# Another table of engine orders for a fused attention and feed-forward kernel

## The chip, the cores and the metric

The kernel runs on one core of a Trainium2 chip. The metric is the device time in microseconds of one execution, as the median of several.

## What is computed

The reference, cut to its core:

```python
# attention: B, H, S, D = 4, 8, 768, 64; n_sink, window = 4, 64
scores = (1 / sqrt(D)) * q @ k.T
causal = rel >= 0                                # rel = query position - key position
stream_keep = causal & (is_sink | (rel < window))
mask = causal for the retrieval heads, stream_keep for the others
a = softmax(where(mask, scores, -1e9));  attn = a @ v
x = attn.transpose(0, 2, 1, 3).reshape(3072, 512)
# feed-forward: w_in [512, 2048], w_out [2048, 512]
h = x @ w_in
g = h - tanh(h)
out = g @ w_out                                  # float32 [3072, 512]
```

Which of the eight heads are retrieval heads is an input (three of them); it is read on the chip, and the masks are made from it.

## The kernel before

The 3072 tokens are worked in twelve tiles of 256, three for each batch. A tile goes through attention (transposes of q and k, scores, exp, masks, scores times v), then the hidden layer (`x @ w_in`, tanh, shrink `h - tanh(h)`), then the output layer. All data for the matmuls is float16.

The work is first recorded and then issued. Each step (four matmuls into a bank, one DVE operation, one transfer) calls `op`, which notes the engine, its expected cost and the function that issues it; there are 1653 such operations. A planner can order them, but a written table `SEQ` takes its place when it isn't empty: `follow` issues the operations in exactly that order, takes the PSUM banks from `BANK` and the lengths of the warm-up fillers from `SIZE`:

```python
for k, x in zip(self.held, BANK):
    self.bank_of[k] = (x, x + 1) if k[0] == "sc" else (x,)
self.size = SIZE
for i in self.seq[a:b]:
    self.ops[i][2]()
```

Each engine works its instructions in the order in which they were issued, so the order on TensorE (PE), VectorE (DVE), ScalarE (ACT), GpSimd (POOL) and in the transfer queues of SyncE (SP) and POOL is `SEQ` cut down to that engine. Waits between engines follow from what an operation reads and writes.

Names and lines that matter here (lines of the kernel before; the kernel after has each of them one higher from line 480 on):

- PE: L2137 `ones` are warm-up fillers, matmuls without a use, in groups with the lengths of `SIZE`. L1339 and L1342 make the matrices for each head, L1241 transposes q and k (the first three tiles), L1366 makes scores, L1450 multiplies them by v, L1546 transposes an attention result `x` (`x16_0` to `x16_3` are the four head pairs of tile 0), L1597 is the hidden layer with `win` (four quarters of w_in), L1670 and L1796 the output layer. From tile 4 on (L1796) the output layer is worked in seven block products, which need sums of blocks of g (L1763, tiles `m`) and of w_out (L1710).
- DVE: L1093 masks from the head flags; L1112 `prod` and its followers rank the heads; L1223 copies out of a bank or casts; L1422, L1404 and L1398 apply masks; L1470 and L1511 (or L1496) divide by the softmax sum; L1622 shrinks; L1763 sums; L1837, L1855 and L1867 take, fold and add the block products into the output tile `ot`.
- ACT: L1385 exp, L1611 tanh, L1221 copies and casts, L1835 takes.
- POOL: casts of q, k, v (L847, L883), the copy `vf` of v for the retrieval heads (L939), the other sums and adds, and the transfers of v, `win` and w_out into the chip.
- SP: the other loads, the transposes by DMA, and the stores of `ot`.

Which engine does an operation that more than one could do stands in small tables of letters, one string for a tile: `CASTS` the first casts of q and k, `TE` and `XE` copies after transposes, `IE` and `OE` further copies, `SUMS` (L1763), `ADDS` (L1867), `TAKES` (L1835 and L1837). D is DVE, A ACT, P POOL.

## Time and profile before

| | |
|---|---|
| median of 3 runs | 223.64 us (223.12 to 224.26) |
| the profiled execution, its own time | 222.99 us |
| its span in the profile | 221.1 us |
| PE busy | 211.8 us, 2468 matmuls |
| DVE busy | 185.8 us |
| POOL busy | 140.9 us |
| ACT busy | 134.9 us |

The span runs from the first instruction to the last; the profiled execution's own time includes what lies around it. PE's busy time includes matmuls that overlap one another at their ends. A wait is put down to what ended last before the engine went on.

### The profile page before, as it was taken

How to read it: one execution, taken by the hardware profiler on the slowest of the kernel's cores; microseconds unless marked ns; L12 is line 12 of the kernel's file. 1: busy time of each engine (PE TensorE's matmuls, PEld its weight loads, DVE VectorE, ACT ScalarE, POOL GpSimd, SP SyncE). 2: the span in 40 equal slices, each digit the busy share in tenths (PEclk: the TensorE clock that was granted, in tenths of full speed). 3: DMA queues.
4: the chain of work that ended last, by engine and by line, in shares of the span. 5: the costliest groups of instructions: out<-in, count | busy, mean ns of one | idle time of the engine just before them, and what ended most of it. 6: DMA issues, size and time to landing. Idle time of an engine off the chain costs nothing.

```text
span 221.1 us, 6568 instructions
## 1 busy us (share of the span) xinstructions
PE 211.8 (96%) x2468; PEld 174.9 (79%) x2468; DVE 185.8 (84%) x462; ACT 134.9 (61%) x214; POOL 140.9 (64%) x270
## 2 busy tenths in 40 slices
PE   7979999999999999999999999999999999999990
PEld 7657888788876675877897988989889888988880
DVE  5789978955889989798999997999897899797972
ACT  4998767885355859754675659456546774634500
POOL 8991985900899368476979999787856840030350
PEclk9999999999999999999999999999999999999999
DMA  6999999999999999999999765949244021051123
GB/s 169 178 202 201 179 175 175 197 211 245 221 187 225 221 205 241 177 233 205 216 266 202 162 144 127 231 79 183 46 89 110 3 47 50 3 142 47 52 96 104
DMA packets 112743, 34.56 MB, mean 156 GB/s; under 512 B 98882, under 2 KB 112194, under 8 KB 112706
## 3 DMA queue, kind: packets, MB, share of 16 engines
q1 hardware_dynamic: 86896, 26.75, 57.5%
q0 software_dynamic: 24992, 6.82, 30.1%
q10 hardware_dynamic: 818, 0.52, 0.8%
q8 instruction: 20, 0.33, 0.6%
q14 instruction: 17, 0.14, 0.2%
HBM read 27.26 MB, written 6.29 MB: 152 GB/s over the span
## 4 chain that ended last, share of the span: by engine, by line
PE 77%; DVE 10%; DMA 6%; ACT 3%; issue 2%; SPq 0%; DVEq 0%; POOLq 0%; POOL 0%; ACTq 0%
PE banks L1597 34%; PE banks L1796 18%; PE banks L1670 9%; PE banks L1366 7%; PE banks L1450 6%; DMA out_dram<-ot 4%; DVE gt L1622 2%; ACT pt L1385 2%; DMA rawqk<-in_k_dram 2%; DVE ot L1855 1%; DVE gu L1622 1%; ACT th L1611 1%; DVE x L1511 1%; DVE m L1763 1%; DVE QK L1223 1%
## 5 line engine op out<-in xcount | busy, mean ns | idle before, releaser
L1597 PE MATMUL banks<-xT,win 128*128 128x256 f16 x768 | 96.2, 273 | 1.3 <-DVE x L1511 1.2
L1597 PEld LDWEIGHTS <-win 128*128 128x128 f16 x768 | 72.5, 98 | 11.9 <-DMA win<-in_moe_w_in_dram 1.2
L1611 ACT ACTIVATE th<-banks 128x512 f32<-128x512 f32 x96 | 55.3, 600 | 43.3 <-PE banks L1597 34.8
L1622 DVE SCALAR_TENSOR_TENSOR gt<-th,banks 128x512 f16<-128x512 f32 x88 | 58.3, 681 | 9.1 <-ACT th L1611 8.2
L1385 ACT ACTIVATE pt<-banks 128x1024 f16<-128x1024 f32 (+3 forms) x57 | 49.3, 901 | 8.7 <-PE banks L1366 8.2
L847 POOL CAST t<-rawqk 128x256 f16 x64 | 25.7, 427 | 21.8 <-PE banks L1450 12.5
L1796 PEld LDWEIGHTS <-m 128*128 128x128 f16 x256 | 24.3, 98 | 3.2 <-issue 0.4
L1670 PE MATMUL banks<-wout,gt 128*128 128x256 f16 (+1 forms) x160 | 26.3, 294 | 0.0
L1496 DVE TENSOR_TENSOR x16t<-banks,rinv 128x128 f32 (+1 forms) x80 | 22.7, 287 | 1.5
L1763 POOL TENSOR_TENSOR m<-gt 128x512 f16<-128x512 f16 x11 | 12.7, 1156 | 17.5 <-DVE gt L1622 15.3
L1385 ACT ACTIVATE ptn<-banks 128x1024 f16<-128x1024 f32 (+1 forms) x18 | 17.2, 953 | 9.2 <-PE banks L1366 8.0
L883 POOL CAST v<-rawv 128x128 f16 x64 | 20.0, 340 | 3.0 <-DMA rawv<-in_v_dram 2.8
L1366 PE MATMUL banks<-QK 64*128 64x128 f16 (+1 forms) x343 | 20.9, 236 | 0.1
L1796 PEld LDWEIGHTS <-gt 128*128 128x128 f16 x192 | 18.2, 98 | 3.2 <-issue 0.5
L1366 PEld LDWEIGHTS <-QK 64*128 64x128 f16 x343 | 13.0, 94 | 6.7 <-issue 5.1
L1796 PE MATMUL banks<-wout,m 128*128 128x256 f16 x128 | 17.9, 273 | 0.0
L1450 PEld LDWEIGHTS <-pt 128*128 128x128 f16 x390 | 16.2, 97 | 2.1 <-issue 0.8
L1796 PE MATMUL banks<-wout,gt 128*128 128x256 f16 x128 | 17.5, 273 | 0.0
L1670 PEld LDWEIGHTS <-gt 128*128 128x128 f16 x160 | 14.2, 98 | 4.1 <-issue 0.7
L1450 PE MATMUL banks<-v,pt 128*128 128x65 f16 x208 | 16.5, 193 | 0.0
L1763 POOL TENSOR_TENSOR m<-gt,m 128x512 f16<-128x512 f16 x11 | 13.6, 1242 | 4.6 <-DVE m L1763 4.6
L1470 DVE RECIPROCAL rinv<-banks 128x4 f32<-128x4 f32 x48 | 8.3, 178 | 7.2 <-PE banks L1450 5.8
(129 smaller groups left out, 324.2 us busy)
## 6 DMA issues: line engine op xcount, KB each, us to landing
rawqk<-in_q_dram SPq DMA_DIRECT2D x18, 256.0 KB, 4.4
out_dram<-ot SPq DMA_DIRECT2D x18, 256.0 KB, 2.7
rawqk<-in_k_dram SPq DMA_DIRECT2D x17, 256.0 KB, 4.4
rawv<-in_v_dram SPq DMA_DIRECT2D x16, 256.0 KB, 4.6
win<-in_moe_w_in_dram POOLq DMA_DIRECT2D x4, 512.0 KB, 9.8
wout<-in_moe_w_out_dram POOLq DMA_DIRECT2D x4, 512.0 KB, 8.7
out_dram<-ot SPq DMA_DIRECT2D x10, 128.0 KB, 3.9
v<-in_v_dram POOLq DMA_DIRECT2D x6, 128.0 KB, 7.1
```

Of the source, the lines that this page charges most:

```text
L847: nc.gpsimd.tensor_copy(out=c5()[:, :, :, s_ : s_ + 1, :], in_=r5()[:, :, :, at, :])
L883: nc.gpsimd.tensor_copy(out=v1s[b]()[:, g * NB : g * NB + NB, RANK[s_] : RANK[s_] + 1, 0:D], in_=rw()[:, :, at, :],)
L1366: nc.tensor.matmul(out=flat[:, 512 * hh + o : 512 * hh + o + nb * 128], lhsT=lhsT, rhs=QK[p_, hp, q_0 : q_0 + nb * 128], start=not added, ...
L1385: nc.scalar.activation(out=o_, in_=i_, func=AF.Exp, scale=inv_sqrt_d)
L1450: nc.tensor.matmul(out=av()[:, i, hh, :], lhsT=pt()[:, hh, co : co + 128], rhs=vv, start=(jb == first_jb[hh]), stop=(jb == qb),)
L1496: nc.vector.tensor_mul(out=xt()[:, :, at, :], in0=av()[:, :, hh : hh + 1, 0:D], in1=rinv()[:, :, hh : hh + 1].unsqueeze(3).to_broadcast([1 ...
L1597: nc.tensor.matmul(out=ph()[:, j, :], lhsT=w_in_t[fb // 4][:, cb, f0 : f0 + 128], rhs=xT()[:, :, cb, :], start=(cb == 0), stop=(cb == HP - 1),
L1611: lambda: nc.scalar.activation(out=th()[:], in_=ph()[:], func=AF.Tanh, scale=1.0 / XS),
L1622: nc.vector.scalar_tensor_tensor(out=o_, in0=a, scalar=-XS, in1=b, op0=ALU.mult, op1=ALU.add,)
L1670: nc.tensor.matmul(out=po()[:, c0:c1], lhsT=gt()[:, f, ts * 128 : ts * 128 + 128], rhs=w_out_t[:, f, c0:c1], start=(f == 0), stop=(f == NF ...
L1763: lambda k=k, fn=fn, a=a, b=b, cs=cs, e=e: getattr(engs[e], fn)(out=S4[k][:, cs, :], in0=a()[:, cs, :], in1=b()[:, cs, :]),
L1796: nc.tensor.matmul(out=po()[:, at : at + CM], lhsT=lhs(c), rhs=rhs(c), start=c == 0, stop=c == NC - 1,)
```

## The change

`SEQ` and `BANK` are replaced as a whole, `SIZE` gets more groups (67 filler matmuls in place of 53), and the tables of letters change, which moves 62 of the 1653 operations to another engine. `SPL`, `SPT` and the 620 that becomes 450 are costs that only the planner reads; with a written `SEQ` they issue nothing and move nothing. The diff, with one row of each long table:

```diff
 SEQ = [
-    0, 1, 14, 3, 2, 4, 15, 7, 17, 5, 10, 16, 13, 18, 8, 9, 6, 11, 38, 12,
...
+    0, 1, 14, 4, 2, 10, 16, 3, 17, 7, 15, 5, 18, 8, 9, 13, 6, 38, 19, 128,
...
 BANK = [
-    7, 7, 6, 5, 4, 0, 2, 6, 2, 1, 0, 4, 5, 1, 7, 7, 2, 5, 3, 3, 1, 0, 1, 2, 4, 1, 0, 0, 0, 0, 0, 0,
...
+    7, 7, 6, 5, 4, 0, 2, 6, 0, 5, 0, 3, 4, 1, 5, 5, 2, 3, 7, 3, 7, 0, 1, 2, 3, 5, 2, 7, 1, 0, 0, 0,
...
-SIZE = {128: 20, 129: 14, 130: 11, 131: 4, 132: 4}
+SIZE = {128: 20, 129: 21, 130: 4, 131: 3, 132: 3, 133: 4, 134: 5, 135: 7}
...
-    TE = (('AA', 'AA', 'AD', 'DD'), ('AA', 'DD', 'AA', 'AA'), ('AA', 'DD', 'AD', 'DD'))
-    XE = ('DDDD', 'DAAD', 'DADA')
+    TE = (('AA', 'AA', 'AA', 'DD'), ('DD', 'AA', 'DA', 'AA'), ('AD', 'AA', 'DD', 'DD'))
+    XE = ('DADD', 'DDAA', 'DADA')
     BYD = 2
+    SPL, SPT = 18.0, 18.0
...
-    CASTS = ('AA', 'AA')
+    CASTS = ('DA', 'DA')
...
-    SUMS = ('DDDDDDDD', 'DDDDDDDD', 'DDDDDDDD', 'DDDDDDDD', 'DDDDPDDP', 'PDPDDPPP', 'PDDDDDPD', 'DDDPPDPP', 'PDPDPPPP', 'PDPDPDDD', 'PDDDDDDP', 'DDPDDDPP')
-    ADDS = ('PPP', 'PPP', 'PPP', 'PPP', 'PPD', 'DPP', 'DPP', 'PDD', 'PPD', 'DDD', 'DPP', 'DPP')
-    TAKES = ('AA', 'AA', 'AA', 'AA', 'AA', 'DA', 'AA', 'AA', 'AA', 'DA', 'AA', 'DD')
+    SUMS = ('DDDDDDDD', 'DDDDDDDD', 'DDDDDDDD', 'DDDDDDDD', 'DDDDPPDP', 'DDDDDDDD', 'DDDDDPPP', 'DPDDPPDP', 'PDPDPPPP', 'DDPDDDPD', 'DPDDDDDD', 'DDDDDDDD')
+    ADDS = ('PPP', 'PPP', 'PPP', 'PPP', 'PPD', 'PPP', 'PPP', 'PPP', 'PDP', 'DPP', 'PPD', 'PPP')
+    TAKES = ('AA', 'AA', 'AA', 'AA', 'AA', 'AA', 'AD', 'AA', 'AA', 'AA', 'DA', 'AA')
...
-    IE = (('AD', 'DA'), ('DA', 'DA'))
+    IE = (('DA', 'AD'), ('DA', 'DA'))
...
-    OE = ('ADDD', 'DDAA', 'AAAA', 'AAAA', 'AAAA', 'AAAA', 'AAAA')
+    OE = ('DDDA', 'DDDD', 'AAAA', 'AAAA', 'AAAA', 'AAAA', 'AAAA')
```

The order on VectorE at the start, ahead of the last attention result of tile 0 (`x_3` is `x16_3`; `m_128` is a mask, `QK` and `xT` are copies of transposes). Before:

```order
L1223 COPY QK_249<-banks 128x2x128
L1223 COPY t_1_319<-t16p_209 128x2x256 x2
L1470 RECIPROCAL rinv_358<-banks 128x4
L1470 RECIPROCAL rinv_363<-banks 128x4
L1511 TENSOR_TENSOR x_1_369<-banks,rinv_358 128x256
L1511 TENSOR_TENSOR x_2_375<-banks,rinv_363 128x256
L1223 COPY xT_378<-banks 128x2x128 x2
L1107 TENSOR_REDUCE iota<-upto 128x8
L1223 COPY xT_378<-banks 128x2x128
L1470 RECIPROCAL rinv_402<-banks 128x4
L1112 TENSOR_TENSOR prod<-upto,rflag 128x64
L1511 TENSOR_TENSOR x_3_420<-banks,rinv_402 128x256
```

The same place after:

```order
L1113 TENSOR_TENSOR prod<-upto,rflag 128x64
L1224 COPY t_1_327<-t16p_209 128x2x256
L1224 COPY xT_369<-banks 128x2x128
L1471 RECIPROCAL rinv_375<-banks 128x4
L1512 TENSOR_TENSOR x_2_383<-banks,rinv_375 128x256
L1471 RECIPROCAL rinv_385<-banks 128x4
L1512 TENSOR_TENSOR x_1_388<-banks,rinv_385 128x256
L1224 COPY QK_259<-banks 128x2x128 x2
L1224 COPY xT_369<-banks 128x2x128
L1471 RECIPROCAL rinv_415<-banks 128x4
L1108 TENSOR_REDUCE iota<-upto 128x8
L1512 TENSOR_TENSOR x_3_437<-banks,rinv_415 128x256
```

`prod` has moved from the row ahead of `x_3` to eleven rows ahead of it, and the two copies of `QK` that followed `x_3` stand before it. Farther ahead (not shown), six masks stand in place of four, and two casts of the first q.

On TensorE, from the transposes of `x_3` to the first matmuls with the second quarter of `win` (`win_145`; `win_144` is the first); a pair of rows that follows itself is shown once. Before:

```order
L1546 LDWEIGHTS x_3_420
L1546 MATMUL banks<-ident_123,x_3_420 128x128
L1597 LDWEIGHTS win_144
L1597 MATMUL banks<-xT_378,win_144 128x256
L1366 LDWEIGHTS QK_249
L1366 MATMUL banks<-QK_249 128x256
L1597 LDWEIGHTS win_145
L1597 MATMUL banks<-xT_378,win_145 128x256
L2137 LDWEIGHTS ones
L2137 MATMUL banks<-ones 128x128
```

After:

```order
L1547 LDWEIGHTS x_3_437
L1547 MATMUL banks<-ident_123,x_3_437 128x128
L1598 LDWEIGHTS win_144
L1598 MATMUL banks<-xT_369,win_144 128x256
L1598 LDWEIGHTS win_145
L1598 MATMUL banks<-xT_369,win_145 128x256
```

Before, two matmuls of the first quarter stand ahead of `x_3` (not shown) and fourteen behind it, then ten of scores, two of the second quarter and four fillers. After, all of the first quarter stands behind `x_3`: twelve, then two of the second quarter, the other four of the first, and then the scores, with no fillers.

On VectorE at the sums of tile 5 (`gt_2167` before and `gt_2178` after are its shrunk hidden layer, `m_128` holds the sums, `pt` and `ptn` are masked weights of attention). Before:

```order
L1622 SCALAR_TENSOR_TENSOR gt_2167<-th_2311,banks 128x512
L1855 SCALAR_TENSOR_TENSOR ot_2374<-banks,ot_2204 128x512
L1763 TENSOR_TENSOR m_128<-gt_2167 128x512
L1763 TENSOR_TENSOR m_128<-m_128,gt_2167 128x512
L1867 TENSOR_TENSOR ot_2204<-gu_1330,ot_2374 128x256
L1404 TENSOR_TENSOR ptn_2401<-ptn_2401,mS 128x1024
L1837 TENSOR_SCALAR gu_1330<-banks 128x512
L1422 TENSOR_TENSOR pt_2382<-pt_2382,m4r 128x2x512
L1855 SCALAR_TENSOR_TENSOR ot_2457<-banks,gu_1330 128x512
```

After:

```order
L1623 SCALAR_TENSOR_TENSOR gt_2178<-th_2306,banks 128x512
L1856 SCALAR_TENSOR_TENSOR ot_2382<-banks,ot_2204 128x512
L1868 TENSOR_TENSOR ot_2204<-gu_1365,ot_2382 128x256
L1764 TENSOR_TENSOR m_128<-gt_2178 128x512 x2
L1423 TENSOR_TENSOR pt_2410<-pt_2410,m4r 128x2x512
L1764 TENSOR_TENSOR m_128<-m_128,gt_2178 128x512 x2
L1764 TENSOR_TENSOR m_128<-gt_2178,m_128 128x512
L1764 TENSOR_TENSOR m_128<-gt_2178 128x512
L1405 TENSOR_TENSOR ptn_2389<-ptn_2389,mS 128x1024
L1856 SCALAR_TENSOR_TENSOR ot_2474<-banks,gu_1365 128x512
```

Six of the sums stand here in place of two, and the take (L1837) is gone from this queue.

8 lines of the change are left out of this document (4 added, 4 removed), and 192 rows, old and new, of tables (BANK, SEQ).

## The prediction

> **What bounds the kernel now.** I read the page first (busy time, the chain), then a table of stretches, then the timeline of TensorE (PE) wherever a stretch was not full.
>
> ```profile
> span 221.1 us, 6568 instructions
> PE 211.8 (96%) x2468; PEld 174.9 (79%) x2468; DVE 185.8 (84%) x462; ACT 134.9 (61%) x214; POOL 140.9 (64%) x270
> ...
> 0.00:20.00 20.00, 16.73 (x208) 13.29 (x209) 15.44 (x60) 15.46 (x29) 15.26 (x28) 1.00 1.35 185
> 20.00:70.00 50.00, 49.31 (x605) 40.63 (x603) 40.27 (x97) 33.24 (x53) 32.34 (x71) 1.00 1.42 200
> 70.00:215.00 145.00, 144.97 (x1654) 120.57 (x1653) 128.46 (x302) 86.17 (x133) 93.22 (x171) 1.00 0.67 140
> 215.00:221.10 6.10, 0.79 (x7) 0.39 (x5) 1.63 (x6) 0.00 (x0) 0.09 (x1) 0.98 0.29 94
> ```
>
> In the table the columns after the stretch's length are the busy times of PE, its weight loads, VectorE (DVE), ScalarE (ACT) and GpSimd (POOL), then the granted clock, 1.00. PE is full from 70 to 215 us (144.97 of 145) and nearly so from 20 to 70 (0.69 idle). What a new order can win lies in three places: 3.27 us idle in the first 20, 0.69 in the next 50, and 5.31 after 215. Order cannot shorten the rest, since the same matmuls run at the same clock; only the warm-up fillers grow in number (53 to 67), and they stand before 20 us. So the sum has three terms: start, middle, tail.
>
> **Start.** The first hidden-layer matmuls (L1597) set the pace:
>
> ```profile
> 15.86 0.38 PE L1597 MATMUL banks<-xT,win 128*128 128x256 f16 x2 [1.23 <-DVE x L1511]
> ...
> 15.47 0.34 DVE x L1511
> ...
> 16.84 1.25 PE banks L1597 x10
> ...
> 18.91 0.22 PE banks L2137 x4
> ```
>
> The first row is PE's timeline, the others are the chain's. PE idles 1.23 us before 15.86. Two things end just then: the last attention tile x16_3 (DVE, ending at 15.81) and the first quarter of w_in, `win`. The first two quarters' issues and landings:
>
> ```profile
> L814 POOL DMA_DIRECT2D win<-in_moe_w_in_dram x2: 780/781/782, 7.5 to 8.2; - x2
> ...
> DMA to landing us min/median/max: 8.1/8.9/9.7
> ```
>
> Quarter 0 lands at 7.5 + 8.1 = 15.6, quarter 1 at 8.2 + 9.7 = 17.9 us. Both are on POOL's queue with the same loads ahead of them in both kernels, so I keep both landings.
>
> *TensorE's order.* Before, all 16 matmuls of quarter 0 run ahead of the first of quarter 1 and are done at 18.1 (16.84 + 1.25). After, only 12 stand ahead of it; two of quarter 1 are followed by the other four, and then the scores. At 0.125 us each (1.25 / 10), the four make 0.50. With quarter 1 at 17.9, after resumes 0.2 earlier than 18.1 but has 0.50 less done: +0.30. The four fillers of 18.91 (0.22) are gone from that place: -0.22. So +0.1 at the least, if the landings hold and nothing else is late.
>
> *VectorE's order ahead of it.* In after, PE's first hidden matmul stands behind x16_3's transposes, and DVE has more ahead of x16_3: two casts that ACT did and two more masks (L1093).
>
> ```profile
> 8.23 0.45 DVE L1223 COPY QK<-banks 128x256 f16<-128x256 f16 x1 [0.57 <-PE banks L1241]
> 10.33 0.18 DVE L1470 RECIPROCAL rinv<-banks 128x4 f32<-128x4 f32 x1 [0.84 <-ACT pt L1385]
> 11.22 0.51 DVE L1223 COPY t<-t16p 128x512 f16<-128x512 f16 x2
> 12.23 0.18 DVE L1470 RECIPROCAL rinv<-banks 128x4 f32<-128x4 f32 x1 [0.41 <-PE banks L1450]
> 14.12 1.35 DVE L1112 TENSOR_TENSOR prod<-upto,rflag 128x64 f32<-128x64 f32 x1
> 17.85 0.22 DVE L1141 TENSOR_TENSOR prod<-pos_b,iota 128x64 f32<-128x64 f32 x1
> ...
> L1093 DVE TENSOR_SCALAR m<-A,thr x8: 347/488/760, 5.0 to 23.9; 128x512 f16<-128x512 f16 x8
> ...
> 14.32 1.06 POOL L939 TENSOR_TENSOR vf<-v,rflag 128x520 f16<-128x520 f16 x1
> ```
>
> A cast (f32 to f16, 128x512) is not on DVE in this trace. Bounds: a f16 copy of that size, 0.51 / 2 = 0.26, and the longest mask, 0.76; I take 0.5, between them, since the cast reads twice the bytes of the copy. The extra work is 2 x 0.5 + 2 x 0.49 = 2.0 us, and DVE's idle ahead of x16_3 0.57 + 0.84 + 0.41 = 1.8. Against this, `prod` (L1112) took 1.35 us at 14.12, beside POOL's `vf` (14.32 to 15.38), where an equal product at 17.85 took 0.22: 1.1 us that after saves if `prod`, now moved ahead, misses POOL. So against before x16_3 comes between 2.0 - 1.8 - 1.1 = -0.9 (all idle used, collision gone) and +2.0 (neither). With half of the idle used it is 0.0 without the collision and +1.1 with it; I take +0.5, between these. An earlier x16_3 is worth nothing while `win` bounds it. Start: +0.1 to +1.1, +0.5 taken; it falls below zero only if `win` lands earlier.
>
> The Trainium skill ("SBUF — State Buffer", section "SBUF: two separate sides") says that VectorE and GpSimd exclude one another at a shared port pair for a whole instruction, where VectorE's reads two SBUF inputs or runs in a two-port mode. `prod` agrees: it ended 0.09 us behind `vf`. By that rule the added casts and masks could each wait for a POOL instruction as well, and the term would be +1.1 rather than +0.5.
>
> The extra fillers of the second batch (14 to 21) run while PE waits for the raw q and k. At ten in 1.27 us (the row below) seven are 0.9 us; they move the per-head matmuls back, but the fillers between the halves of the first transposes shrink from 11 to 4, and the first scores wait for ACT's copies. I cost them at nothing; without that cover they cost 0.9.
>
> ```profile
> 3.71 1.27 PE L2137 MATMUL banks<-ones 128*128 128x128 f16 x10
> ```
>
> **Middle.** The largest single gap after 20 us, from the chain:
>
> ```profile
> 62.48 0.69 DVE gu L1622
> 63.17 1.26 DVE t L1710
> 64.43 1.21 DVE gu L1622 x2
> ...
> 65.68 1.04 PE banks L1670 x4
> ```
>
> Weight sums for the output scheme (L1710) stood 1.26 us between shrinks that PE needed. After has another order there, so this gap may vanish, for a gain of at most 0.7 (the table's idle from 20 to 215 us is 0.69 + 0.03). A like gap of 0.7 may open elsewhere, one or another. The tightest place is tile 5, whose eight sums of gt (L1763) all go to DVE, five of them from POOL:
>
> ```profile
> 112.00:130.00 18.00, 18.00 (x221) 15.70 (x219) 16.79 (x38) 11.45 (x19) 16.54 (x26) 1.00 0.93 178
> ...
> L1763 DVE TENSOR_TENSOR m<-gt x21: 396/420/1111, 98.2 to 211.2; 128x512 f16<-128x512 f16 x21
> ...
> 117.29 0.61 DVE L1763 TENSOR_TENSOR m<-gt 128x512 f16<-128x512 f16 x1
> 117.93 1.26 DVE L1763 TENSOR_TENSOR m<-m,gt 128x512 f16<-128x512 f16 x1
> 119.12 0.73 DVE L1867 TENSOR_TENSOR ot<-gu,ot 128x256 f32<-128x256 f32 x1
> ...
> 120.52 0.68 DVE L1837 TENSOR_SCALAR gu<-banks 128x512 f32<-128x512 f32 x1
> ```
>
> DVE has 18 - 16.79 = 1.2 us of room. Five more sums at the median 0.42 make +2.1; the take (0.68) and the add (0.73) leave DVE, and the two sums here fall from 1.87 to 0.84 if no POOL sum runs beside them: 2.1 - 0.68 - 0.73 - 1.03 = -0.3. What hides the added sums is that PE has other tiles' matmuls queued; without it a late sum costs PE its lateness. Over all tiles eight sums go to DVE (8 x 0.42 = 3.4) and seven adds and two takes leave it (7 x 0.42 and 2 x 0.68, 4.3 off), so its load hardly moves. Middle: 0, from -0.7 to +0.8, the upper end being one new gap like the old one.
>
> **Tail.**
>
> ```profile
> 211.28 2.46 DMA out_dram<-ot
> ...
> 213.86 0.43 DVE ot L1855
> ...
> 214.39 0.42 DVE gu L1855
> 214.82 0.34 DVE ot L1867
> ...
> 215.25 0.79 DVE ot L1855 x3
> 216.04 1.77 DMA out_dram<-ot
> ...
> L1867 POOL TENSOR_TENSOR ot<-gu,ot x6: 720/728/905, 115.8 to 211.6; 128x256 f32<-128x256 f32 x6
> ```
>
> A fold waits for the store that frees its buffer (sent 211.28), then fold, fold, add and folds follow, and the last store ends it. The buffer is reused in the same way after. Tile 11's sums go to DVE (three from POOL), its two takes to ACT, its add (L1867) to POOL. The takes ended before the fold that waits, so they give nothing. The add leaves DVE's chain (-0.34); on POOL it takes 0.73, hidden behind the two folds of 0.42 that stand there between its input and the fold that reads it; without that cover it costs 0.73 - 0.34 = 0.4. The folds may also stand for PE's last piece, which gives the gain back. Tail: -0.2, from -0.34 to +0.4.
>
> **Sum.** +0.5 + 0 - 0.2 = +0.3 on the profiled execution, 222.99 us (span 221.1). That one lies 0.65 under the median of the runs, so on the median 223.64 + 0.3 = 223.9. About 0.5% (1.1 us) is what a measurement can tell from no change: 222.5 to 224.8.
>
> **Rivals.** (a) *Slower: VectorE becomes late at tile 5.* The traces show a sum stretching from 0.42 to 1.26 beside POOL, and POOL is busy 16.54 of 18 us there. If each of the eight sums takes half of that stretch, 0.84, they cost 6.7 against the 0.40 + 0.61 + 1.26 = 2.3 (the low end of the sums' row for the third) before; less take and add, +3.0, less the room of 1.2: 1.8 us late, which PE pays when its queue has nothing else: 223.9 + 1.8 = 225.7. It decides from a mean of about 0.6 per sum (8 x 0.61 - 2.3 - 1.4 = 1.2). Against it: most of POOL's work there would be casts, shorter than its sums. Chance 0.25. The page just named would have every sum blocked until POOL's instruction ends; it gives this rival and no other number.
>
> (b) *Faster: the start gains.* x16_3 comes 0.9 earlier and quarter 0 lands earlier with it: start -0.5. With the gap at 65.68 closed (-0.7) and the tail's -0.2 that is 223.64 - 1.4 = 222.2. It takes a landing before 15.1; instruction fetches travel on the same 16 DMA engines, 20 packets in all, and shift with the 14 extra fillers, so a landing may move by some tenths either way. Against it: the bytes ahead of `win` are the same.
>
> ```profile
> q8 instruction: 20, 0.33, 0.6%
> ```
>
> Chance 0.22. The Trainium skill ("Runtime: NRT & Kernel Launch", section "Instruction fetch mechanics") has blocks of 256 instructions fetched and says that crossing one is mostly hidden; the 20 packets fit with 2 x 2468 PE instructions, and hidden means no change.
>
> (c) *The orders differ but nothing moves by more than the measurement tells*, my forecast: PE is 100% busy for 145 of 221 us under both. Chance 0.53.
>
> **How the numbers follow.** Likeliest 223.9; its own range 222.8 to 224.8. The three terms at their ends together reach -0.9 and +2.3 (222.7 and 225.9); with (b) at 222.2 and (a) at 225.7, and about a tenth cut on each side, the range is 222.1 to 225.6. Faster by over 0.5%: 0.22, slower: 0.25, within: 0.53.
>
> **What would show it.** Start: the first L1597 matmul at 16.0 to 17.0 in after, the first of quarter 1 not before 17.9, x16_3 (L1512 there) ending 16.0 to 16.9, `prod` at 0.2 if it missed POOL. Middle: PE idle from 20 to 215 us still under 1.5, and another place than 65.68; tile 5's sums near 0.42 in the mean (rival a: 0.8, and idle PE near 125 us). Tail: last PE piece to end of span 5.4 us or less, against 221.1 - 215.5 = 5.6. The prediction fails if a transfer lands a microsecond earlier or later than I kept it, or if the new order of the loads on SP's queue makes PE wait in a place that was full.

## The result, and the profile after

After took 229.79 us (median of 4 runs, 228.95 to 230.48), before 223.89 in the same job (223.12 to 224.26): a ratio of 1.0266, 95% interval 1.0219 to 1.0314. The change makes the kernel 2.7% slower, 4.2 us beyond the upper end of the forecast range. The profiled execution of after took 228.95 us, span 227.2, 6.1 us more span than before. A ratio below leaves out executions more than 1.5% above the fastest of the same kernel (one of run 13's twelve, two of run 14's six; run 3, with two of four, has no ratio), while medians and ranges hold all.

The page of after (first rows), then the same stretches as in the prediction's first fence:

```profile
span 227.2 us, 6598 instructions
PE 214.1 (94%) x2482; PEld 176.8 (78%) x2482; DVE 188.2 (83%) x464; ACT 134.6 (59%) x213; POOL 136.7 (60%) x269
...
0.00:20.00 20.00, 15.02 (x176) 11.80 (x177) 16.19 (x48) 10.86 (x22) 18.84 (x32) 0.91 1.34 181
20.00:70.00 50.00, 49.63 (x630) 41.91 (x628) 37.36 (x104) 34.92 (x55) 26.71 (x63) 1.00 1.42 184
70.00:215.00 145.00, 143.43 (x1628) 118.00 (x1627) 129.15 (x298) 88.05 (x136) 90.09 (x174) 1.00 0.68 142
215.00:227.20 12.20, 6.03 (x55) 5.09 (x53) 5.55 (x15) 0.76 (x2) 1.07 (x3) 0.83 0.28 91
```

TensorE was busy 1.71 us less in the first 20 us (15.02 against 16.73), at a mean clock of 0.91, and 1.57 us of idle time have appeared between 70 and 215 us, where before had 0.03.

Busy time alone does not say how far TensorE has come, since fillers and half-clock matmuls are busy too. So below a *lag* is worked out: each matmul other than a filler counts with the median distance to the next one of its kind in before (197.2 us in all), and the time at which a kernel has done w us of them is set against the time at which before had. A last column compares the spans. Before's profiled execution lies 0.65 us under its median and after's 0.84 under its own, so the two compare.

| lag of after against before, us | w = 5 | w = 30 | w = 80 | w = 100 | w = 190 | span |
|---|---|---|---|---|---|---|
| after | +5.4 | +4.2 | +4.1 | +5.5 | +5.2 | +6.1 |

So 4.2 of the 6.1 us are lost in the start; between w = 30 and 60 the lag falls to 2.8 (before's own gaps, the one at 65.68 among them, are gone); 2.7 are lost again from 80 to 118 us of the clock; the end costs 0.9.

**The start of after.** VectorE's timeline, then GpSimd's in the same stretch, and last the row of x16_0 in before:

```profile
9.18 1.84 DVE L1082 TENSOR_SCALAR t<-ident,coef 128x128 f16<-128x128 f16 x1
10.95 0.34 DVE L1094 TENSOR_SCALAR m<-A,thr 128x512 f16<-128x512 f16 x1
...
11.29 1.59 DVE L1082 TENSOR_SCALAR t<-ident,coef 128x128 f16<-128x128 f16 x1
11.45 1.43 DVE L1224 COPY QK<-banks 128x256 f16<-128x256 f16 x1
11.78 2.31 DVE L1094 TENSOR_SCALAR m<-A,thr 128x512 f16<-128x512 f16 x2
...
14.11 1.04 DVE L1224 COPY t<-t16p 128x512 f16<-128x512 f16 x1
15.08 0.41 DVE L1512 TENSOR_TENSOR x<-banks,rinv 128x256 f16<-128x256 f32 x1
15.41 0.21 DVE L1113 TENSOR_TENSOR prod<-upto,rflag 128x64 f32<-128x64 f32 x1
15.54 0.30 DVE L1224 COPY t<-t16p 128x512 f16<-128x512 f16 x1
...
9.88 1.09 POOL L940 TENSOR_TENSOR vf<-v,rflag 128x520 f16<-128x520 f16 x1
10.88 0.95 POOL L667 DMA_DIRECT2D v<-in_v_dram  x1
11.84 0.31 POOL L963 TENSOR_SCALAR_AFFINE_SELECT upto<-ones 128x64 f32<-128x64 f16 x1
12.08 0.77 POOL L815 DMA_DIRECT2D win<-in_moe_w_in_dram  x1
12.87 2.13 POOL L940 TENSOR_TENSOR vf<-v,rflag 128x520 f16<-128x520 f16 x2
...
10.54 0.42 DVE L1511 TENSOR_TENSOR x<-banks,rinv 128x256 f16<-128x256 f32 x1
```

Read the ends. The head matrix that began at 9.18 ended at 11.02, 0.05 behind `vf` (10.97). The next ended at 12.88, 0.03 behind the issue of `win` (12.85). The two masks ended at 14.09, the copy of `t` at 15.15, 0.15 behind the second `vf` of the last row (15.00). An equal mask took 0.34 (at 10.95), an equal copy 0.30 (at 15.54), and a head matrix 0.24 in a run below. Beyond that stood 1.60 + 1.35 + (2.31 - 0.68 =) 1.63 + 0.74, less 1.10 in which two of them stood at once (11.78 to 12.88): 4.2 us, or 3.8 if the own 0.43 of the copy of QK that lies among them counts as work. x16_0, the `x` at 15.08, comes behind them all and ended at 15.49, in before at 10.96: these stalls are most of its 4.5 us. (The lag of 4.2 at w = 30 is another quantity: between the two lie what `prod` saved and the lowered clock below.) Not every transfer issue held VectorE: the mask at 10.95 ran beside the issue of `v`, the copy at 15.54 beside one of `win`. `x`, which reads PSUM, took 0.41 as ever; the copy of QK at 11.45, which does too, waited behind the head matrix.

TensorE's gaps and its first hidden-layer matmul, from its timeline, and the clock in three stretches:

```profile
12.93 0.34 PE L1340 MATMUL banks<-t 128*128 128x384 f16 x1 [1.40 <-DVE QK L1224]
15.54 0.39 PE L1547 MATMUL banks<-ident,x 128*128 128x128 f16 x2 [1.13 <-DVE x L1512]
...
19.88 0.38 PE L1598 MATMUL banks<-xT,win 128*128 128x256 f16 x2
...
12.00:15.00 3.00, 1.49 (x16) 0.68 (x16) 3.00 (x6) 1.31 (x2) 2.98 (x5) 0.96 1.26 208
15.00:18.00 3.00, 2.46 (x29) 2.46 (x30) 2.55 (x11) 1.16 (x3) 3.00 (x5) 0.50 1.55 192
18.00:20.00 2.00, 2.00 (x38) 1.72 (x37) 1.67 (x8) 1.66 (x5) 2.00 (x3) 0.95 1.29 204
```

The first hidden matmul comes 4.02 us later than before's (15.86). While TensorE waited (1.49 busy of 3.00), the granted clock fell, to 0.50 from 15 to 18 us. The Trainium skill ("TensorE: Matmul & The Clock Gate", section "What's actually happening") has the clock halved after an idle window; these rows agree as far as half speed followed the waits, so that waiting costs twice, once as a gap and once as half speed behind it. But TensorE was not idle throughout here, and in run 5 a wait of 1.82 us left the clock at 1.00. How much of the start's lag is the clock's, no run separates.

**From 80 to 118 us.** TensorE's longest waits there, from its timeline:

```profile
92.60 0.61 PE L1598 MATMUL banks<-xT,win 128*128 128x256 f16 x4 [0.60 <-DMA xT<-x16t]
114.94 0.56 PE L1367 MATMUL banks<-QK 64*128 64x256 f16 x10 [0.56 <-DVE gt L1623]
```

Idle time is 1.57 us of the 2.7 that are lost here; the rest is not explained.

**The end.** DVE's last fold that waits, and its last operation (a memset behind the last store), then TensorE's last matmul:

```profile
219.70 0.42 DVE L1856 SCALAR_TENSOR_TENSOR ot<-banks,gu 128x256 f32<-128x256 f32 x1 [1.44 <-DMA out_dram<-ot]
...
223.50 0.06 DVE L1969 MEMSET ot<- 1x2 f32 x1 [1.34 <-DMA out_dram<-ot]
...
224.12 0.16 PE L1975 MATMUL banks<-ot 1*2 1x2 f16 x1 [3.26 <-DVEq L2280]
```

### The profile page after: what moved, and what is told of

Same layout as the page of the kernel before. It is cut to its first block, busy times and chain, and to the rows that moved or that the text cites. A ratio compares the mean times of both kernels' runs of the same rounds, so it can differ in the third digit from the quotient of the medians.

```text
span 227.2 us, 6598 instructions
## 1 busy us (share of the span) xinstructions
PE 214.1 (94%) x2482; PEld 176.8 (78%) x2482; DVE 188.2 (83%) x464; ACT 134.6 (59%) x213; POOL 136.7 (60%) x269
## 4 chain that ended last, share of the span: by engine, by line
PE 73%; DVE 13%; DMA 6%; ACT 3%; issue 2%; SPq 0%; DVEq 0%; POOLq 0%; ACTq 0%; POOL 0%
PE banks L1598 31%; PE banks L1797 16%; PE banks L1671 10%; PE banks L1367 6%; PE banks L1451 6%; DVE gt L1623 4%; DMA xT<-x16t 2%; DMA rawqk<-in_k_dram 2%; DMA out_dram<-ot 2%; DVE m L1764 2%; ACT pt L1386 1%; DVE t L1082 1%; DVE ot L1856 1%; DVE wout L1711 1%; PE banks L1242 1%
## 5 line engine op out<-in xcount | busy, mean ns | idle before, releaser
L1623 DVE SCALAR_TENSOR_TENSOR gt<-th,banks 128x512 f16<-128x512 f32 x88 | 57.5, 679 | 6.6 <-ACT th L1612 6.4
L848 POOL CAST t<-rawqk 128x256 f16 x64 | 27.8, 459 | 20.9 <-DMA rawqk<-in_q_dram 13.6
L884 POOL CAST v<-rawv 128x128 f16 x64 | 18.8, 322 | 12.8 <-DMA rawv<-in_v_dram 12.6
L1367 PE MATMUL banks<-QK 64*128 64x128 f16 (+1 forms) x343 | 21.4, 236 | 0.9 <-DVE gt L1623 0.6
L1868 POOL TENSOR_TENSOR ot<-gu,ot 128x256 f32<-128x256 f32 x11 | 8.6, 785 | 17.1 <-ACT gu L1836 12.0
L1451 PEld LDWEIGHTS <-pt 128*128 128x128 f16 x390 | 17.4, 99 | 1.9 <-issue 0.5
L1451 PE MATMUL banks<-v,pt 128*128 128x65 f16 x208 | 17.3, 196 | 0.1
L1797 PE MATMUL banks<-wout,m 128*128 128x256 f16 x128 | 17.1, 273 | 0.0
L1423 DVE TENSOR_TENSOR pt<-pt,m4r 128x1024 f16<-128x1024 f16 (+1 forms) x18 | 12.9, 716 | 1.1 <-ACT pt L1386 1.0
```

The source lines that it names most:

```text
L848: nc.gpsimd.tensor_copy(out=c5()[:, :, :, s_ : s_ + 1, :], in_=r5()[:, :, :, at, :])
L884: nc.gpsimd.tensor_copy(out=v1s[b]()[:, g * NB : g * NB + NB, RANK[s_] : RANK[s_] + 1, 0:D], in_=rw()[:, :, at, :],)
L1367: nc.tensor.matmul(out=flat[:, 512 * hh + o : 512 * hh + o + nb * 128], lhsT=lhsT, rhs=QK[p_, hp, q_0 : q_0 + nb * 128], start=not added, ...
L1423: nc.vector.tensor_mul(out=pv, in0=pv, in1=m)
L1451: nc.tensor.matmul(out=av()[:, i, hh, :], lhsT=pt()[:, hh, co : co + 128], rhs=vv, start=(jb == first_jb[hh]), stop=(jb == qb),)
L1623: nc.vector.scalar_tensor_tensor(out=o_, in0=a, scalar=-XS, in1=b, op0=ALU.mult, op1=ALU.add,)
```

## The experiments

Operations are named by their number in `SEQ`. Two theories of the start run through the first eight runs. **L**: VectorE's operations from SBUF to SBUF stand still while GpSimd works, its transfer issues included. **W**: VectorE has more work ahead of x16_3, and that is all. Each run is given with its median, the range and, where there were several, the ratio to before with its interval.

### 1. The casts go back to ScalarE

```diff
-    CASTS = ('DA', 'DA')
+    CASTS = ('AA', 'AA')
```

> The kernel after with one letter table as before: the first two casts of q go back to ScalarE (CASTS AA). Theory L (lock): VectorE's operations that read only SBUF stand still while GpSimd works, and the two casts (0.85 and 0.83 us) push the last head matrices and masks into GpSimd's vf and transfer issues (1.84, 1.59, 1.2 and 1.0 us in place of some 0.3 each). Without the casts most of them run ahead of vf: the first hidden matmul goes from 19.9 to about 16.5 us, the time from 229.8 to about 226.4. Theory W (work): the casts are 1.7 us more work on VectorE and nothing else: first hidden matmul 18.2, time 228.1.

228.52 us (227.92 to 229.99), ratio 1.0248 (1.0195 to 1.0301). Taking 1.7 us of casts off VectorE did not bring the first hidden matmul forward: 20.64 us. Two masks now stood where head matrices had:

```profile
8.83 2.29 DVE L1094 TENSOR_SCALAR m<-A,thr 128x512 f16<-128x512 f16 x2
...
12.40 2.97 DVE L1094 TENSOR_SCALAR m<-A,thr 128x512 f16<-128x512 f16 x2
```

W falls. L's own number falls too: I had expected the earlier masks to slip through between GpSimd's operations.

### 2. GpSimd's vf moved behind its transfer issues

```diff
 SEQ, GpSimd's part
-... 63, 67, 218, 64, 85, 68, 126, 127, 66, 69 ...
+... 63, 67, 64, 85, 68, 66, 69, 218, 126, 127 ...
```

> The kernel after with GpSimd's three operations vf (L940) of batch 0 moved behind the issue of the first quarter of w_out; nothing moved on VectorE, which keeps its casts. Theory L (lock): the head matrices and masks take 0.25 to 0.35 us again and the first hidden matmul comes at about 17 us, time 226.8. If the transfer issues hold VectorE too, the matrix that ran 1.59 us beside them stays long and half of the gain is left, 228.2. Theory W (work): VectorE has the same work, so the first hidden matmul stays at 19.9 and the time at 229.8.

228.37 us (227.51 to 230.9), ratio 1.0248 (1.0171 to 1.0325). The head matrices are quick again, where they had stood 1.84 and 1.59; the stalls moved to what now lies beside the issues (the last two rows are GpSimd's):

```profile
9.17 0.23 DVE L1082 TENSOR_SCALAR t<-ident,coef 128x128 f16<-128x128 f16 x1
...
9.99 0.24 DVE L1082 TENSOR_SCALAR t<-ident,coef 128x128 f16<-128x128 f16 x1
...
10.49 1.53 DVE L1094 TENSOR_SCALAR m<-A,thr 128x512 f16<-128x512 f16 x2
...
12.03 1.50 DVE L1224 COPY t<-t16p 128x512 f16<-128x512 f16 x1
...
10.98 1.55 POOL L815 DMA_DIRECT2D win<-in_moe_w_in_dram  x2
12.47 0.94 POOL L826 DMA_DIRECT2D wout<-in_moe_w_out_dram  x1
```

The copy ended at 13.53, 0.12 behind the issue of `wout` (13.41). First hidden matmul 18.68, 1.2 earlier: L's half gain (228.2), not W's 229.8, though the range is wide. The first matrix began at the same time as in after (9.18), beside the same issues of `win`; only the `vf` behind those was gone. So in after it was `vf` that held it, though that operation's recorded start (9.88) is 0.70 later than the matrix's. That issues can hold VectorE up is seen here; that they always do is not (run 12).

### 3 and 4. Two repairs of the waits at 92 and 115 us

Run 3 moves two transfers of SyncE (a load, 640, and a store, 596) behind the transpose xT of tile 4 (666); run 4 moves two sums (920, 925) behind the shrink 945.

```diff
 SEQ, run 3: SyncE
-... 640 ... 596 ... 666 ...
+... 666, 640, 596 ...
 SEQ, run 4: VectorE
-... 920 ... 925, 945 ...
+... 945, 920, 925 ...
```

> The kernel after with one load of q (tile 5) and one store on SP's queue moved behind the transposes xT of tile 4. Theory Q (queue): xT was issued at 87.50, 2.06 us after its input was ready, because loads and a store stood ahead of it at about 1 us each; now it is issued at about 85.5 and the wait of 0.76 us at 92.60 is gone: time 229.0. Rival: the transposes land behind the bytes of the loads whenever they are issued (5.05 us for a median of 3.1): landing and wait stay, 229.8.

> The kernel after with two weight sums (L1711, the fifth and sixth of the second set) moved on VectorE behind four shrinks and a fold of tile 5 that TensorE waits for. Theory L: one of them stood 1.21 us beside GpSimd instead of 0.28; with the shrinks ahead the gaps of 0.72 at 114.94 and 0.29 at 116.69 close, and the sums are still in time for the products at 118.8: time 228.8. Rival: VectorE is full there, and the lateness goes on to the products that read the weight sums: no change, 229.8.

Run 3: 231.09 us (227.72 to 231.96), a spread too wide to place its time. In its profile the wait for xT at 92.60 was gone, but a fold waited 1.82 us, to 114.03, and TensorE waited 1.5 us for the first shrink behind it and 1.2 for the next. The profile puts the fold's wait down to TensorE; it ended as a store landed that was issued at 109.37, not the one moved (88.11), and that took 4.5 us where the one of 109.45 in after took 3.0. Run 4: 229.08 (228.62 to 229.19), ratio 1.0246 (1.0211 to 1.0281), which cannot be told from after's 1.0266 nor from the 228.8 expected: the same fold waited 1.63 us in the place of the sums, again to the landing of that store (4.1 us). That store is an inference from the times. In both profiles a local repair there only handed the wait on.

### 5 and 6. VectorE's masks moved out of GpSimd's way

```diff
 SEQ, run 5: VectorE
-... 46, 118, 123, 49, 124, 24, 50, 45, 121, 119, 96, 62, 97, 235, 59 ... 115 ...
+... 46, 49, 50, 24, 45, 96, 97, 62, 59 ... 115, 118, 123, 124, 121, 119, 235 ...
 SEQ, run 6: run 5, and 640 behind 666, 920 and 925 behind 945, the store 828 ahead of 763
```

> The kernel after with VectorE's order at the start changed and nothing else moved: the last two head matrices (L1082) right behind the first copy of QK, five masks (L1094) and prod behind the last attention result of tile 0, x16_0 ahead of the copy of t. The casts stay on VectorE and GpSimd's vf where they are. Theory L (lock): what stood 1.2 to 2.3 us beside GpSimd no longer stands ahead of x16_0 to x16_3, so x16_0 comes near 11.5 instead of 15.1 and the first hidden matmul near 16.5 instead of 19.9; time 229.8 - 3.4 = 226.4, and the lowered clock of 14 to 19 us is gone. Theory W (work): only the masks' own 5 x 0.34 = 1.7 us are saved: first hidden matmul 18.2, time 228.1.

> The start of the run before (masks later), and in the middle: on SP's queue a load of q behind the transposes xT of tile 4, and the store of the output tile ot of slot 1 ahead of two transposes instead of behind them (its data were ready 17 us earlier); on VectorE two weight sums behind the shrinks of tile 5. The theory is that the gaps near 92 and 114 to 118 us (0.76, 0.72 and 0.29 in the kernel after, up to 1.6 and 1.3 in runs that came to that place earlier) are SP's queue and these VectorE waits. They close: 1.3 to 2 us under the run before, about 224.6. Rival: the gaps at 114 to 118 us come from the scores and the hidden matmuls waiting on shrinks that are late for another reason; then they stay and the time is within 0.5 us of the run before.

Run 5: 226.89 us (225.94 to 229.01), ratio 1.0163 (1.0110 to 1.0216); x16_0 begins at 11.32 (15.08 in after), x16_3 at 16.43 (19.01), first hidden matmul at 17.11, clock 1.00 up to 20 us. With every other engine's order as in after, placing ten operations elsewhere on one engine gave back 2.9 us, near L's 226.4 and not W's 228.1. What was left at the start, from TensorE's timeline and VectorE's:

```profile
14.13 0.62 PE L1242 MATMUL banks<-ident,t 128*128 128x128 f16 x8 [1.05 <-DVE t L1224]
19.74 1.47 PE L1598 MATMUL banks<-xT,win 128*128 128x256 f16 x12 [1.82 <-DVE xT L1224]
...
11.67 2.41 DVE L1224 COPY t<-t16p 128x512 f16<-128x512 f16 x2
```

The copies of `t` (0.3 each when free) now stood beside `vf`, and the five masks stood ahead of a copy of xT: my own doing. Run 6: 230.14 (228.88 to 231.34), ratio 1.0283 (1.0236 to 1.0329); as run 5 up to 112 us, then a wait of 2.3 us for a masked `ptn` that no order of mine had foreseen. A miss.

### 7 and 8. The reverse, on before

```diff
 SEQ, run 7: VectorE of before
-... 111, 234, 105, 114, 235, 115 ...      ... 622 ... 506 ...
+... 111, 105, 114, 115, 234, 235 ...      ... 506, 622 ...
 SEQ, run 8: VectorE of before
-... 43, 96 ... 239, 119, 240, 121 ...
+... 43, 49, 50, 121, 119, 96 ...
```

> The kernel before with two moves on VectorE: prod and iota (L1107, L1112) behind the last attention result of tile 0, and one weight sum (L1710) that stood 1.26 us ahead of two shrinks at 63.1 us behind them. If these two collisions with GpSimd cost TensorE what the trace of before showed (up to 0.7 in the start, since the first quarter of win lands at 15.6, and 0.5 at 65.68), the time falls from 223.6 to about 222.5. Rival: the start is held by win and a later wait takes the place of the gap at 65.68: 223.6.

> The kernel before with one part of the change: two masks (L1093) and the last two head matrices (L1081) put on VectorE ahead of the first attention result of tile 0, near where the kernel after has them; GpSimd's order stays. Theory L (lock): one or more of them stand beside vf (10.3 to 11.4 us) or a transfer issue for about 1 us, so x16_0 comes 1 us or more later and the first hidden matmul at 16.9 or later; time 224.6 to 225.5. Theory W (work): 2 x 0.34 + 2 x 0.24 = 1.2 us fit into VectorE's idle of 0.84 and 0.41 there: first hidden matmul at 15.9 to 16.0, time 223.6.

Run 7: 223.62 us (222.73 to 224.25), ratio 0.9992 (0.9973 to 1.0012). `prod`, which still took 0.91, now stands behind x16_3, and the first hidden matmul comes at 15.40 (15.86), yet a gap of 0.71 at 55.40 and smaller ones later take it back: the rival's number. Run 8: 223.72 us (223.25 to 225.2), ratio 1.0002 (0.9982 to 1.0022). Here L's number was wrong: the two masks took 0.69 at 9.72, just ahead of `vf` at 10.34, so there was no collision. Run 8 is thus the control for run 12.

### 9 to 11. One stretch at a time

The two tables can be joined: the first N operations of one, then the rest of the other in its order, each operation with its own engine letter and bank.

```diff
 SEQ, BANK, SIZE and the engine letters
+run 9:  before's first 310 operations (TensorE at 39 us), then after's order
+run 10: after's first 315 operations (TensorE at 43 us), then before's order
+run 11: before's first 1165 operations (TensorE at 142 us), then after's order
```

> The kernel before up to its 310th operation (TensorE at about 39 us there), with its engine letters, PSUM banks and 53 fillers, and the rest in the order of after. Theory S (the loss is a sum of separate stretches; the start is worth what the progress of TensorE shows, 4.0 to 4.1 us): 229.8 - 4.1 = 225.7 us; the first hidden matmul stands near 15.9 again, the clock is 1.00 throughout, and the stalls of after between 85 and 118 us (about 1.5 us of added lag) are still there. Rival D (what the start loses is only the front of a queue: VectorE stays the bound of after's later order, and the time comes back as waits at 105 to 118 us): 228 or more, with the waits there 2 us longer. Rival T (the losses after 80 us are a consequence of the late start: collisions that fall differently): 223.9 to 224.5.

> The other way round: after's first 315 operations (TensorE at about 43 us), with its letters, banks and 67 fillers, and the rest in the order of before. Theory S: 223.9 + 4.1 = 228.0 us (before's own stalls at 43.95, 55.45 and 65.68 may go or stay: 226.7 to 228.0), with the first hidden matmul at 19.9 and the clock down to 0.50 in 15 to 18 us. Rival D: the order of before catches up, 225 or less. Rival T: 229.8, all of the loss.

> The kernel before up to its 1165th operation (TensorE at about 142 us), the rest in the order of after. It tells what the end costs alone: from 215 us to the end after took 0.9 us longer than before. Theory S: 223.9 + 0.7 to 0.9 = 224.6 to 224.8 us, with TensorE's last piece 6.3 to 6.6 us ahead of the end. Rival: the end is longer in after only because its clock or its phase was another; then 223.9 and 5.7 us.

| run | median, range | ratio to before, interval | lag at w = 5 | 30 | 80 | 100 | 190 | span |
|---|---|---|---|---|---|---|---|---|
| 9, start of before | 224.06 (223.09 to 225.57) | 1.0006 (0.9981 to 1.0030) | 0.0 | 0.0 | -1.0 | -0.5 | -0.8 | +0.2 |
| 10, start of after | 226.80 (226.32 to 227.70) | 1.0127 (1.0105 to 1.0149) | +5.4 | +5.5 | +4.7 | +5.1 | +5.1 | +4.9 |
| 11, end of after | 225.78 (225.66 to 225.96) | 1.0078 (1.0064 to 1.0091) | -0.1 | 0.0 | +0.5 | +1.0 | +1.1 | +3.0 |

Run 9 is the main result: with before's first 39 us, all the rest of after's order costs nothing that can be measured. The row of the windows for 80 to 120 us, first of after, then of run 9:

```profile
80.00:120.00 40.00, 38.43 (x433) 28.73 (x432) 36.78 (x95) 24.55 (x39) 29.10 (x73) 1.00 1.14 216
...
80.00:120.00 40.00, 39.86 (x453) 30.62 (x453) 37.85 (x95) 26.20 (x41) 29.86 (x69) 1.00 1.08 216
```

1.57 us of idle time there against 0.14: the same order of that stretch, entered on time, did not wait. But the parts do not add up. The start alone costs 2.8 us (226.80 - 223.97), the rest alone 0.1, both together 5.9. Theory S, which had them add up, expected 1.6 us more in run 9; in run 10 the time lies at the low end of its 226.7 to 228.0. Rival T's number came in run 9, but not its 229.8 in run 10. (Run 10's profile was of its slowest execution, 0.9 us over its median, so its lags look larger than its cost.) Some 3 us arise only where after's start and after's later order come together, and runs 15 to 17 below show that even then they need not. Run 11 I can't fully explain, and neither expectation had its time: 0.5 and 0.4 us of its lag appeared in stretches that are before's own, and its waiting fold waited 2.09 us for its store instead of 1.44.

### 12. Three masks moved on before

```diff
 SEQ, VectorE of before
-... 36, 118, 122 ... 96, 97, 46, 60, 61 ... 239, 119, 240, 121 ...
+... 36, 122 ... 96, 97, 118, 119, 121, 46, 60, 61 ... 239, 240 ...
```

> One part of the change done alone on the kernel before: three of its masks (SBUF to SBUF, 0.35 us each when free) are moved on VectorE to stand right behind x16_0 (which ended at 10.97), beside GpSimd's vf (10.32 to 11.38), a transfer issue of win (11.32 to 12.14) and the next vf (12.24 to 13.28). Theory L (such an operation stands still while GpSimd works, its transfer issues too): each mask ends within 0.2 us of the end of a GpSimd operation, so the three end near 13.3 and not 12.0, the copy of QK behind them ends at 13.7, and the first hidden matmul comes 1.5 to 2.4 us later; 225.0 to 226.2 us. Rival W (it is only work in the way): the three take 1.05 us, of which 0.4 are idle time of VectorE, the first hidden matmul is 0.5 later: 224.2 us.

228.14 us (228.12 to 229.55), ratio 1.0201 (1.0174 to 1.0228): 4.2 us for three operations of 0.35 on an engine that is 84% busy, no instruction added or taken away. VectorE's timeline, then GpSimd's, then TensorE's gaps:

```profile
10.93 1.41 DVE L1093 TENSOR_SCALAR m<-A,thr 128x512 f16<-128x512 f16 x3
12.26 0.43 DVE L1223 COPY QK<-banks 128x256 f16<-128x256 f16 x1
12.59 2.98 DVE L1223 COPY t<-t16p 128x512 f16<-128x512 f16 x2
...
10.43 1.05 POOL L939 TENSOR_TENSOR vf<-v,rflag 128x520 f16<-128x520 f16 x1
11.43 0.82 POOL L814 DMA_DIRECT2D win<-in_moe_w_in_dram  x1
12.27 1.07 POOL L939 TENSOR_TENSOR vf<-v,rflag 128x520 f16<-128x520 f16 x1
...
14.35 1.06 POOL L939 TENSOR_TENSOR vf<-v,rflag 128x520 f16<-128x520 f16 x1
...
12.74 0.34 PE L1366 MATMUL banks<-QK 64*128 64x256 f16 x4 [1.37 <-DVE QK L1223]
15.62 0.51 PE L1241 MATMUL banks<-ident,t 128*128 128x128 f16 x6 [1.56 <-DVE t L1223]
```

The masks themselves lost little (1.41 for 1.05): they were not held through the whole issue of `win`, against L's expectation. But they pushed the two copies of `t`, 0.51 together before, from the place behind one `vf` (beside an issue of `win` that let them pass) into the next two: 2.98 us, ending at 15.57, 0.16 behind a `vf` (15.41). The first hidden matmul came at 18.74, 2.9 later. The lag is +3.4 at w = 30 and +5.3 at w = 100, like after's. W had 0.5, L 2.4 at the most. So in the start a displacement of one microsecond became more than three, by what it displaced; the other 1.9 of the lag came between w = 40 and 100, in stretches whose order is before's own, and why is not shown.

### 13. After's middle alone

```diff
 SEQ, BANK and the engine letters
+before's first 310 operations, after's order up to its 1371st (TensorE at 174 us), then before's order
```

> Before's first 310 operations and before's end, and between them (TensorE at about 39 to 174 us) the order of after, with its letters and banks. The run with before's start alone gained 0.7 to 1.2 us on before between 40 and 75 us and lost 0.9 at the end. Theory S (the stretches add up): 223.97 - 0.7 = 223.3 us, with the end 5.5 to 5.8 us behind TensorE's last piece. Rival: the end of after is not what costs, and the profiled gain is chance: 223.9 to 224.1 us, as with before's start alone.

224.27 us (222.93 to 226.28), ratio 1.0021 (0.9990 to 1.0053). No gain: the rival's number, if anything worse. Its profile has a lag of -0.5 at w = 70 and +0.2 from w = 100 on, where run 9's had -1.1 and -0.5; the gain that I had read from run 9's profile does not show in the times, and no version here beats before.

### 14. The masks behind the last copies

```diff
 SEQ, VectorE of after
+49, 50, 24 behind 46; 96, 97 ahead of 62; 235 behind 115; 118, 119 behind 179; 121, 123, 124 behind 163
```

> After, with TensorE's, ScalarE's, GpSimd's and SyncE's orders, letters and fillers as they are. On VectorE alone: head matrices 49 and 50 right behind the first QK copy, x16_0 ahead of the t copies, prod behind x16_3, masks 118 and 119 behind the last xT and QK copies of the start, and 121, 123 and 124 behind the first product pt*m. An earlier run that moved the masks only as far as x16_3 came to 226.89 us and had TensorE wait 1.98 us at 19.74 for a copy of xT that stood behind five masks. Theory L with its remainder (that wait was the five masks in the way of the copy; the 1.05 us at 14.13 for the t copies beside vf stay): 226.9 - 1.8 = 225.1 us, first hidden matmul at 17.1, lag at 30 us 1.3 to 1.6. Rival (TensorE's order, the casts or the fillers are what costs the start): 226.9 or more, since none of these is touched.

228.75 us (225.69 to 231.37), ratio 1.0182 (1.0129 to 1.0234), a spread too wide to place. The profile is of the slowest execution, so only its start is read: first hidden matmul at 17.13, no wait for xT (the wait of 1.82 is gone, as expected), lag +1.4 at w = 8 and +2.8 at w = 30 where 1.3 to 1.6 was expected, with new waits of 0.45 at 19.05 for the second quarter of `win` and 0.30 at 22.18 for a `pt`. The total is inconclusive.

### 15 to 17. Fewer fillers

```diff
-SIZE = {128: 20, 129: 21, 130: 4, 131: 3, 132: 3, 133: 4, 134: 5, 135: 7}
+SIZE = {128: 20, 129: 14, 130: 4, 131: 3, 132: 3, 133: 1, 134: 1, 135: 1}   # run 15
+SIZE = {128: 20, 129: 14, 130: 4, 131: 3, 132: 3, 133: 4, 134: 5, 135: 7}   # run 16
+SIZE = {128: 20, 129: 21, 130: 4, 131: 3, 132: 3, 133: 1, 134: 1, 135: 1}   # run 17
```

> After with 47 warm-up fillers for 67: the second batch 14 for 21, and the three last batches (4, 5 and 7, at 14.02, 17.13 and 18.55 us, of which the last two ran at half clock) one each. It leaves out only matmuls of ones that nothing reads. Theory L (they run while TensorE waits for VectorE's x and t in any case): 229.8 us, within 0.3, first hidden matmul 19.5 to 19.9. Rival F (the fillers behind 17 us stand in the way of a late start): 10 fewer at 0.08 to 0.15 us each, 0.8 to 1.5 us off: 228.3 to 229.0 us. Rival C (fewer fillers let the clock fall further): the granted clock under 0.50 or for longer than 15 to 18 us, 230.3 or more.

> After with the second warm-up batch (ahead of 6 us) of 14 fillers for 21, the later batches as they are. The run with 20 fwer fillers in all had the same start as after (first hidden matmul 19.94, lag at 30 us +4.2) and yet came to 226.94 us, since the waits at 92, 115 and 117 us were gone. Theory P (these waits are collisions of transfers, sums and waits whose fall depends on small shifts, not on any one batch): the start stays at +4.0 to +4.3, and the time lies anywhere from 226.5 to 230.5, with the two parts not adding up to the 2.85 us of the whole. Rival F (the late batches at 14 to 19 us were what stood in the way): no change here, 229.8. Rival E (the early batch was): 226.9.

> After with one filler each for the 4, 5 and 7 of the last three batches (14.02, 17.13 and 18.55 us), the second batch as it is (21). Theory P: the start at +4.0 to +4.3, the time anywhere from 226.5 to 230.5, with waits in the profile at 92 and 112 to 118 us that the run with 20 fewer fillers did not have, or none. Rival F: 226.9. Rival E: 229.8.

| run | median, range | ratio to before, interval | lag at w = 30 | 80 | 100 | 190 |
|---|---|---|---|---|---|---|
| 15, 20 fewer | 226.94 (226.26 to 227.68) | 1.0155 (1.0114 to 1.0195) | +4.2 | +2.9 | +3.1 | +3.1 |
| 16, 7 early ones fewer | 227.82 (227.13 to 228.12) | 1.0185 (1.0144 to 1.0226) | +5.4 | +4.0 | +4.2 | +3.9 |
| 17, 13 late ones fewer | 226.71 (226.16 to 227.19) | 1.0135 (1.0094 to 1.0176) | +4.5 | +3.2 | +3.3 | +3.0 |

The start gains nothing: first hidden matmul at 19.94, 20.80 and 20.14 (19.88). In runs 16 and 17 it is later, and the clock stays at half for longer; run 16 against after's rows above, then two rows of run 10, which has after's start with all 67 fillers:

```profile
12.00:15.00 3.00, 1.99 (x16) 0.84 (x16) 3.00 (x6) 1.25 (x2) 2.98 (x5) 0.74 1.19 182
15.00:18.00 3.00, 2.46 (x29) 2.47 (x30) 2.54 (x11) 1.24 (x3) 3.00 (x4) 0.50 1.41 191
18.00:20.00 2.00, 2.00 (x24) 1.74 (x24) 1.70 (x8) 1.36 (x4) 2.00 (x3) 0.50 1.43 195
...
15.00:18.00 3.00, 2.46 (x29) 2.47 (x30) 2.55 (x11) 1.15 (x3) 3.00 (x4) 0.50 1.51 192
18.00:20.00 2.00, 2.00 (x24) 1.74 (x24) 1.70 (x8) 1.35 (x4) 2.00 (x3) 0.50 1.34 202
```

So the longer half clock does not come from fewer fillers: run 10 has it with all of them (first hidden matmul 21.21), and run 15, with the fewest, was back at 0.76 from 18 to 20 us. What decides its length is not shown.

Yet each came out 2.0 to 3.1 us under after, since none of them waits between 80 and 120 us. Run 15, and run 17 the same (40.00 of 40.00):

```profile
80.00:120.00 40.00, 40.00 (x471) 30.77 (x469) 37.14 (x101) 24.72 (x40) 31.50 (x76) 1.00 1.04 206
```

Seven early fillers do it, thirteen late ones do it, and both together do no more than one. So neither batch stood in the way: F's number came in run 17 and failed in run 16, E's came in neither, and none of run 15's theories had a time under 228.3. Theory P had the times, in a range wide enough for nearly any, but not the starts of +4.0 to +4.3 in runs 16 and 17. That a small shift of the later work is what ends the waits is not shown either: from w = 30 to 60 run 15's lag is after's within 0.1 us, and only then do they part. What differs there stays open: the number of TensorE's instructions ahead of that stretch changes too, and these runs do not part the two.

## Why the prediction was wrong, point by point

**Start, +0.5 taken, +4.2 measured: the step that failed.** It is the sum by which x16_3 comes between -0.9 and +2.0 against before; it came 3.6 later (ending at 19.43 against 15.81). Its collision term was the one collision that before's trace showed, `prod`, priced as a gain of 1.1. That held: `prod` took 0.21 in after. But I let the added casts and masks run at their mean and left everything that after *moved* at its old duration: two head matrices, two masks and a copy of `t` came to stand beside three `vf` and the issues between them, and stood some 4 us. Run 12 shows that a displacement of this kind alone costs the kernel before 4.2 us, 3.4 of it by the lag of the start, run 5 that taking it away gives 2.9 back, run 9 that without after's start nothing is lost. The Trainium skill ("SBUF — State Buffer", section "SBUF: two separate sides") states the exclusion; this case's rows agree where an operation stood, with ends 0.03 to 0.16 behind GpSimd's; but some operations passed inside a transfer issue. I had applied it to the two casts and two masks, which gave +1.1, and not to each operation of that form in the new order. The chance of 0.25 for "slower" stood on another place.

**Casts**, 0.5 each: 0.85 and 0.83. Too low, but taking them off VectorE did not bring the first hidden matmul forward (run 1).

**Clock.** The prediction kept it at 1.00. Half clock from 15 to 18 us lies within the start's loss, by how much is not separated; the prediction had no term for it.

**Fillers, "I cost them at nothing":** right at the start (run 15, +4.2 as after), wrong in the sum: with 7 to 20 fewer of them the time was 2.0 to 3.1 us shorter, by waits between 80 and 120 us that went. No term had that, and how the fillers come into it stays open.

**TensorE's own order and the landings**, +0.1: not reached, since nothing waited for `win` at 19.88. But the landings that I kept moved: the first two issues began at 8.38, not 7.49, behind other GpSimd work, and run 14, which got there at 17.13, waited for the second quarter until 19.05, not 17.9. An earlier x16_3 would have met that.

**Middle, 0 (from -0.7 to +0.8).** The gap at 65.68 went, as allowed, and the lag fell by 1.3 up to w = 60. Then 2.7 came back from 80 to 118 us, beyond the upper end. It was not rival (a): the sums from 117 to 126 us, where tile 5's stand, took 0.41 to 0.42 each, and TensorE did not wait behind them. It was xT, issued at 87.50 behind loads and a store though its input was ready at 85.4, and a late shrink. The prediction's last sentence had named "the new order of the loads on SP's queue". Runs 9, 15, 16 and 17 show that the order itself can be run through without that wait. So the sum also failed in taking start and middle as terms that add: by the runs' medians the start alone costs 2.8, the rest alone 0.1, both 5.9.

**Tail, -0.2 (from -0.34 to +0.4).** The chain did what was said: from the waiting fold to the last memset 4.09 us before (213.86 to 217.95), 3.80 after, -0.29. But against the end of TensorE's last piece the fold stood 0.6 later (1.77 ahead of it before, 213.86 against 214.59 + 1.04; 1.17 ahead after, 219.70 against 220.27 + 0.60), and TensorE's closing matmul came 0.62 behind the memset where before's came 0.12 (218.07). That is 0.6 - 0.3 + 0.5 = 0.8 of the 0.9. The last half microsecond also appears in runs 5, 9 and 11, which have after's end (run 9: memset 217.62, matmul 218.24); why is not shown.

**Rivals.** (a) had the sign, not the place. (b) needed `win` to land earlier; nothing waited for it. (c), the forecast, rested on TensorE being full for 145 us "under both", which is what a late start took away.

## What to carry to other kernels

Where a reordering is judged from a trace, list every operation of the engine pair that excludes one another and see what stands beside what in the new order, moved ones as much as added ones; a price taken from the old neighbours is no price. Ask what a displaced operation lands in: three masks of 0.35 us cost 4.2 here, most of it by the two copies behind them. And test a loss by joining the old table's front to the new one's rest, since parts that each cost little can cost more together.

## What the runs showed of the hardware that was not expected

- A VectorE copy or mask from SBUF to SBUF (0.30 to 0.35 us) took up to 1.50 us in a row of its own, and two copies 2.98, while GpSimd worked; operations that read PSUM beside the same GpSimd work kept their 0.41 to 0.44. GpSimd's transfer issues held VectorE up in some places (12.03 for 1.50 in run 2) and let operations pass in others (run 12, three masks in 1.41; in after a mask in 0.34 and a copy in 0.30).
- Two waits of TensorE of 1.40 and 1.13 us were followed by 3 us at a granted clock of 0.50; in runs 10, 16 and 17 the clock stayed there from 15 to 20 us and beyond, with as many fillers as after in run 10 and fewer in the others. In run 5 a wait of 1.82 us did not lower it.
- Taking away seven matmuls that nobody reads, ahead of 6 us, made the kernel 2.0 us shorter, through waits at 92 and 115 us that were gone; by what way is open.
